# Attention with weighed outputs and turned tiles by VectorE and DMA, in an infini-attention plus mixer kernel on one core

## The chip, the core and the metric

The kernel runs on one core of a Trainium2 chip, as one launch. A core has TensorE (PE, matmuls and transposes into PSUM), VectorE (DVE), ScalarE (ACT), GpSimd (POOL), SyncE (SP), whose queue issues most of the DMAs here, and 16 DMA engines. Each engine runs its own instruction stream in order; semaphores tie the streams together. The metric is device time in microseconds for one run of the whole kernel, the median of the runs shown.

## The reference: what is computed

The input x has 2048 tokens of width 1024. First comes attention with a compressive memory, in four segments of 512 tokens and 32 heads of width 32, then a channel MLP. Cut to what matters:

```python
q, k, v = heads(layernorm(x) @ wq), ...          # 32 heads, 4 segments of L = 512
M, z = 0, 0
for s in range(4):
    p = softmax(qs @ ks.T * scale + mask)        # within the segment; mask adds -1e9 above the diagonal
    a_dot = p @ vs
    a_mem = (phi(qs) @ M) / (phi(qs) @ z + 1e-6) # phi(t) = t + 1 for t > 0, else exp(t)
    o_s = g * a_mem + (1 - g) * a_dot            # g = sigmoid(beta), one number a head
    M = M + phi(ks).T @ vs
    z = z + sum(phi(ks))
h = x + concat(o) @ wo
out = h + gelu(layernorm(layernorm(h)) @ w1 + b1) @ w2 + b2
```

A row of the softmax is divided by its sum. That division, and the factor (1 - g), can be applied to each probability or, later, to each output row p @ v: the result is the same.

## The kernel before, in words

The work goes through two halves of 1024 tokens; each half does attention (`attention`), the wo product (`wo_first`, `wo_second`) and the first product of the MLP (`Mixer`). The second product (`Second`) follows at the end. Everything is fp32, carried as a rounded upper part and a lower part (names ending in h and l), so that a product is three matmuls (`mm3`): high by high, high by low, low by high.

Attention of a half walks over 8 groups g of four heads and, inside, over 2 slices sl of 512 tokens. One (g, sl) is a unit: 16 units a half, 32 in all. A unit belongs to segment s = 2 * half + sl. Units with s > 0 read the memory, units with s < 3 update it, so 24 do each.

- `dense` is the projection part of a unit, as a generator of 24 steps: eight steps each for keys, queries and values (`project`), one `mm3` a step. It copies the results out of PSUM into halves (kh, kl, qh, ql), makes phi(keys) (pk) and phi(queries) (pq), and builds the operands of the logits with `stack`: for each of the four heads a 96-row tile of three 32-row blocks, each block copied from SBUF to SBUF by its own DMA, so 12 DMAs for keys and 12 for queries. `late`, which runs inside the next unit, turns the values on TensorE (vt to PSUM vn, then vs in halves), reads the memory (pm, then om), turns what it read on TensorE (om to pom, copied to omt), and updates the memory (pmm). phi(keys) is turned on TensorE too (pk to pkn).
- `heads` runs the softmax part of the unit before, one `slot` of six steps for each of its four heads. `PLAN` says which operations stand in which step: q0 to q3 the logits of the four row blocks (`qk`, with the exponential in `soft`), n the division of two row blocks (`norm`: a reciprocal on VectorE, then a product on GpSimd with the inverse sum and 1 - g), t the transposes of the probabilities on TensorE (`ptr`), s and S the lower halves (`sub`), a the product with the values (`av`), o the addition of its two parts into ot (`av_out`), and at the fourth head the memory's part omt and the store to o_dram. t works on the head one slot back, a on the one two slots back.
- `interleave` weaves the 24 steps of one unit's `dense` with the 24 steps of the previous unit's `heads`.
- `small` is a list of small matmuls (pm and pmm); `one_small` slips one of them in between others.
- `weights` loads wk, wq and wv of the next group (128 columns each) and splits them; `load_o` fetches the outputs of the other groups back from DRAM for the wo product. At the end of a half `last` runs the remaining `heads` beside `wo_first`.

The order of instructions on each engine in this stage isn't the order of the code. A planner goes through the code once, with costs of its own, and puts an instruction on its engine when its inputs and buffers are there by those costs; the place in the code is the priority. The resulting order is fixed before the run. Only some stages (`in_order`) and some single instructions (`behind`, `add_manual_dep`) are tied to the order of the code. Buffers matter to that order: stacks have 5 for each of keys and queries, rounded temporaries (tmpr) 6, plain ones (tmp) 5, PSUM tiles of tag d 3, qk 2, pt 2, av 1.

## Time and profile before

| | |
|---|---|
| Runs | 2302.54, 2303.82 and 2304.96 us; median 2303.82 |
| Profiled execution | span 2296.2 us from the first to the last instruction; its time from outside isn't given separately, the median lies 7.6 us above the span |
| TensorE | busy 2270.4 us, 99% of the span, granted clock 1.000 |
| DVE, ACT, POOL busy | 1540.3, 1225.0, 1092.4 us |
| DMA | 355.36 MB, mean 155 GB/s |
| Stages | attention about 30 to 530 us and 884 to 1400 us; first MLP product to 884 and 1736 us; second MLP product to the end |

How to read the lines that follow in the prediction: a group's row (line, engine, operation, output<-input, shape, count) gives busy microseconds, mean nanoseconds of one, then the idle time of that engine just ahead of these instructions and what ended it. A row of the timeline gives start and duration in microseconds. Matmuls are pipelined, so durations of neighbours on PE overlap, and the cost of one is the distance between starts. A row of a stretch gives its bounds and length, busy time and count of PE, PEld, DVE, ACT and POOL, the granted clock, the DMA share and GB/s. A DMA row gives the count, the size and the median time from issue to landing. SPq and ACTq are the queues of SP and ACT on which DMAs are issued.

### The profile page before, as it was taken

Reading aid. Unit: us, or ns where it says so; the run is one execution under the profiler, and the core shown is the slowest. Engines: PE = TensorE matmul, PEld = TensorE weight load, DVE = VectorE, ACT = ScalarE, POOL = GpSimd, SP = SyncE. Lnnn points to the kernel's source line nnn. Section 1 sums busy time; section 2 is a strip of 40 time slices with the busy share of each in tenths; the row PEclk is TensorE's granted clock in tenths of the full one; section 3 lists DMA queues with packets and bytes.
Section 4 is the critical chain, followed back from the end, with each engine's and each line's share of the span. In section 5 each row is a group of like instructions: output and inputs, shape, how many; then the busy total and the mean of one; then the engine's idle time right before and its main releaser. Section 6 shows DMA issues by size and latency. Waiting matters only on the chain.

```text
span 2296.2 us, 35279 instructions
## 1 busy us (share of the span) xinstructions
PE 2270.4 (99%) x11769; PEld 1890.8 (82%) x11769; DVE 1540.3 (67%) x3173; ACT 1225.0 (53%) x2549; POOL 1092.4 (48%) x1134
## 2 busy tenths in 40 slices
PE   8999999999999999999999999999999999999999
PEld 6888888878888888888888887888888888888887
DVE  6777777776655565777777777565566766577563
ACT  6777777775453445777777776363344223322221
POOL 5545555555244442555555556253445554155430
PEclk9999999999999999999999999999999999999999
DMA  6333333345465654433333344466667976476762
GB/s 190 92 85 91 93 89 85 87 120 182 139 204 172 188 165 142 113 91 86 85 87 88 87 111 140 156 211 175 176 188 263 345 243 216 159 253 221 249 234 90
DMA packets 322719, 355.36 MB, mean 155 GB/s; under 512 B 26190, under 2 KB 218730, under 8 KB 322538
## 3 DMA queue, kind: packets, MB, share of 16 engines
q1 hardware_dynamic: 259370, 316.40, 45.4%
q10 hardware_dynamic: 63168, 36.71, 5.3%
q8 instruction: 93, 1.52, 0.3%
q14 instruction: 88, 0.72, 0.1%
HBM read 226.59 MB, written 76.09 MB: 132 GB/s over the span
## 4 chain that ended last, share of the span: by engine, by line
PE 91%; ACT 3%; POOL 2%; DVE 2%; issue 1%; DMA 1%; ACTq 0%; SPq 0%; POOLq 0%; DVEq 0%
PE po L1278 22%; PE bps L882 9%; PE cps L882 7%; PE dps L882 6%; PE po L593 6%; PE ppt L573 6%; PE pqk L541 3%; PE vps L116 2%; PE vps L115 2%; PE kps L115 2%; PE kps L116 2%; PE vps L117 2%; PE kps L117 2%; PE pwo L117 2%; PE pwo L116 2%; PE pwo L115 2%
## 5 line engine op out<-in xcount | busy, mean ns | idle before, releaser
L557 POOL TENSOR_SCALAR pr<-pr,nm,gate 128x128 f32<-128x128 f32 (+3 forms) x512 | 322.6, 639 | 345.9 <-DVE nm L554 260.0
L550 ACT ACTIVATE pr<-pr,mx 128x256 f32<-128x256 f32 (+3 forms) x512 | 287.6, 562 | 161.9 <-DVE mx L542 158.2
L580 DVE TENSOR_TENSOR ptl<-ppt,pth 128x512 fp32r<-128x512 f32 (+1 forms) x384 | 227.2, 599 | 86.2 <-ACT pth L575 82.0
L542 DVE CUSTOM_DVE_ANT_0 pr<-pqk,mask 128x256 f32<-128x256 f32 (+3 forms) x512 | 243.3, 484 | 46.5 <-PE pqk L541 43.7
L573 PE MATMUL ppt<-ident,pr 128*128 128x128 f32 x1280 | 223.6, 277 | 2.1 <-POOL pr L557 1.4
L575 ACT CAST pth<-ppt 128x512 fp32r<-128x512 f32 (+1 forms) x384 | 194.2, 517 | 39.0 <-PE ppt L573 33.1
L1288 DVE TENSOR_TENSOR c<-c,po 128x512 f32<-128x512 f32 x160 | 105.4, 683 | 143.1 <-PE po L1278 135.5
L573 PEld LDWEIGHTS ppt<-ident,pr 128*128 128x128 f32 x1280 | 164.6, 140 | 32.5 <-POOL pr L557 2.6
L541 PE MATMUL pqk<-ks,qs 96*128 96x256 f32 (+3 forms) x512 | 161.3, 315 | 0.0
L92 POOL TENSOR_TENSOR wl<-wr,wh 128x1024 fp32r<-128x1024 f32 x52 | 124.5, 2393 | 70.8 <-PE pqk L541 27.6
L593 PE MATMUL po<-pth,vs 128*64 128x512 f32 (+3 forms) x512 | 155.4, 326 | 0.3 <-ACT pth L575 0.2
L593 PE MATMUL po<-ptl,vs 128*64 128x512 f32 (+3 forms) x512 | 153.9, 310 | 1.3 <-DVE ptl L580 1.2
L1278 PE MATMUL po<-w2h,zh 128*128 128x512 f32 x378 | 121.1, 390 | 0.8 <-DVE zh L1218 0.4
L1135 POOL TENSOR_TENSOR w2r<-w2r 128x512 f32<-128x512 f32 x54 | 85.4, 1593 | 72.0 <-DVE c L1288 36.9
L541 PEld LDWEIGHTS pqk<-ks,qs 96*128 96x128 f32 x512 | 96.2, 188 | 21.5
L994 POOL TENSOR_TENSOR s<-r 128x512 f32<-128x512 f32 x28 | 43.6, 1559 | 143.4 <-DVE sa L1010 87.1
L882 PE MATMUL bps<-zh,sb 128*128 128x512 f32 x336 | 111.0, 391 | 0.0
L882 PE MATMUL bps<-zh,sa 128*128 128x512 f32 x336 | 110.8, 390 | 0.0
L115 PE MATMUL vps<-yh,wh 128*128 128x512 f32 x256 | 109.4, 427 | 0.9 <-DVE MZ L497 0.9
L115 PE MATMUL kps<-yh,wh 128*128 128x512 f32 (+1 forms) x264 | 110.1, 417 | 0.0
L115 PE MATMUL qps<-yh,wh 128*128 128x512 f32 x256 | 106.8, 417 | 0.0
L1278 PE MATMUL po<-w2h,hl 128*128 128x512 f32 x322 | 103.2, 390 | 0.5 <-POOL hl L1218 0.3
(241 smaller groups left out, 6657.1 us busy)
## 6 DMA issues: line engine op xcount, KB each, us to landing
hr<-h_dram SPq DMA_DIRECT2D x112, 448.0 KB, 5.4
w2r<-in_B_w SPq DMA_DIRECT2D x122, 256.0 KB, 4.4
r<-in_B_w SPq DMA_DIRECT2D x56, 512.0 KB, 4.5
h_dram<-ht ACTq DMA_DIRECT2D x84, 256.0 KB, 3.7
ks<-kh SPq DMA_DIRECT2D x256, 64.0 KB, 2.0
qs<-qh SPq DMA_DIRECT2D x256, 64.0 KB, 2.0
wr<-in_A_wo SPq DMA_DIRECT2D x32, 512.0 KB, 4.0
wx<-in_B_w SPq DMA_DIRECT2D x56, 256.0 KB, 3.5
```

What stands on the lines that cost most here:

```text
L115: nc.tensor.matmul(ps, ah, bh, start=first, stop=False)
L116: nc.tensor.matmul(ps, ah, bl, start=False, stop=False)
L541: nc.tensor.matmul(pqk[:, :n], u["qs"][j][:, i * P:(i + 1) * P], u["ks"][j][:, 0:n], start=True, stop=True)
L542: nc.vector.tensor_tensor_reduce(out=st["pr"][:, offs[i]:offs[i] + n], in0=pqk[:, :n], in1=mask[:, 512 - n:512], op0=ALU.add, op1=ALU.min, ...
L550: nc.scalar.activation(pi, pi, AF.Exp, bias=mx[:, i:i + 1], scale=-1.0, accum_out=mx[:, 4 + i:5 + i])
L557: nc.gpsimd.tensor_scalar(pi, pi, nm[:, 4 + k:5 + k], gate[:, 1, 4 * g + j:4 * g + j + 1], op0=ALU.mult, op1=ALU.mult)
L573: nc.tensor.transpose(ppt[:, o:o + P], pr[:, offs[i] + jk * P:offs[i] + (jk + 1) * P], ident)
L575: acts["pth"] = n, nc.scalar.copy(pth[:, base:base + w], ppt[:, :w])
L580: nc.vector.tensor_tensor(o, x0, x1, op=ALU.subtract)
L593: nc.tensor.matmul(po[:, P * jk:], v, st[part][:, koff[jk]:koff[jk] + w], start=(jk, part) == (0, "pth"), stop=(jk, part) == (2, "ptl"))
L882: nc.tensor.matmul(ps, x_[:, c, :], y_[:, c, :], start=first and c == 0 and n == 0, stop=last and c == 3 and n == 2, skip_group_check=True)
L1278: nc.tensor.matmul(ps, x_[:, k], y_[k], start=opens and k == 0 and i == 0, stop=closes and k == self.KP - 1 and i == 2, skip_group_check=True)
```

## The change

Seven things are changed, all in attention.

1. The softmax isn't divided row by row any more. `norm` is gone; `inverse` (r) takes the reciprocals of a head's four row sums into rs and, at the fourth head, multiplies them by 1 - g on GpSimd. `weigh` (w) turns these 16 columns by one transpose on TensorE (pw), copies them out on ScalarE, stores them to DRAM and reads them back as a 128 x 512 tile in four broadcast loads. `av_out` multiplies the finished ot by it.
2. Values, phi(keys) and retrieved values aren't turned on TensorE any more. `turned` does a VectorE transpose of 32 x 32 blocks, one store to DRAM and four loads that put the blocks in place. The flags VT, KT and OT choose it, and all are on. The order of columns changes with it, so vs, pkh and pkl are indexed anew and omt is added through a rearranged view. The scratch for this lies in the two zt tiles that `wo_first` and `wo_second` use for weights.
3. `stack` stores the three blocks to one DRAM tile (three DMAs of 128 rows) and loads each head's 96 rows with one DMA: 7 DMAs in place of 12.
4. Lower halves of values and phi(keys) move from VectorE to GpSimd.
5. The output store stands at a step of its own (`out_store`, step 62), later than before.
6. Weights are loaded and split at steps (`load_weight`, `cast_weight`); the upper parts of wk and wv are cast on ScalarE, that of wq on VectorE.
7. `late` is gone. `TIMES` gives each operation of a unit a step, counted from the unit's first; 24 and above fall into the next units. `PLAN` is new.

The diff, cut to its core:

```diff
-PLAN = ('q1 S2', 'q0 n0 a0', 'q2 t0 a1', 'q3 n2 s0 o', 't1', 's1 t2')
+VT, KT, OT = True, True, True
+WLC = 8
+TIMES = dict(pk=10, kx=15, pkh=21, pkl=22, ks=16, qs=16, pq=16, pqh=20, pql=20, omt=20, vx=24, pm=25, vs=32, vl=33, pmm=40, om=35, omc=40, od=62, lk=13, lq=16, lv=20, ck=18, cq=22, cv=28)
+PLAN = ('r', 'q0', 'a0 S2 t0 q2 s0', 'a1 q1', 't1 w q3', 't2 o s1')
...
+    PKL, VSL, GTE, WHK, WHQ, WHV = nc.gpsimd, nc.gpsimd, nc.gpsimd, nc.scalar, nc.vector, nc.scalar
...
+        scr = [acts["zt"].tile([P, 4, 512], F32, tag=f"t{x_}3", name=f"sc{x_}") for x_ in "hl"]
+        def turned(src, to, mid):
+            nc.vector.transpose(mid.rearrange("p (c k d) -> p c k d", c=4, k=4), src.rearrange("p (k c d) -> p c k d", c=4, k=4))
+            d = turn_dram[acts.get("turned", 0) % len(turn_dram)]
+            acts["turned"] = acts.get("turned", 0) + 1
+            nc.sync.dma_start(d, mid)
+            for c in range(4):
+                nc.sync.dma_start(to[32 * c:32 * c + 32].rearrange("j (h x) -> j h x", h=4),
+                                  d[:, c * P:(c + 1) * P].rearrange("(h j) x -> j h x", h=4))
...
         def stack(a, b, name, order):
             out = []
+            n = acts[name] = acts.get(name, 0) + 1
+            d = s_dram[name][n % 2]
+            for blk, src in enumerate(order):
+                nc.sync.dma_start(d[:, blk], raw((a, b)[src]))
             for j in range(4):
                 st = ab.tile([96, 512], F32R, tag=name, name=name, bufs=5)
-                for blk, src in enumerate(order):
-                    nc.sync.dma_start(raw(st[32 * blk:32 * blk + 32, :]), raw((a, b)[src][32 * j:32 * j + 32, :]))
+                nc.sync.dma_start(raw(st), d[32 * j:32 * j + 32].rearrange("r b n -> (r b) n"))
                 out.append(st)
...
+            def key_turn():
+                v["kn"] = scr[1][:, 2 + sl]
+                turned(v["pk"], v["kn"], scr[1][:, 0])
+            def key_halves():
+                v["pkh"], v["pkl"] = tmpr("pkh"), tmpr("pkl")
+                v["pkn"] = v["kn"].rearrange("p (h k d) -> p k h d", h=4, k=4)
+                v["pk4"] = [x_.rearrange("p (k h d) -> p k h d", h=4, k=4) for x_ in (v["pkh"], v["pkl"])]
+                nc.scalar.copy(v["pk4"][0], v["pkn"])
+            def value_turn():
+                v["vn"] = scr[0][:, 2 + sl]
+                turned(ps["v"], v["vn"], scr[0][:, 0])
+            def memory_turn():
+                while v.get("read") != 1:
+                    one_small()
+                turned(v["om"], u["omt"], tmp("omx"))
...
-        def norm(st, i):
-            pr, mx, nm, j, g = st["pr"], st["mx"], st["nm"], st["j"], st["u"]["g"]
-            nc.vector.reciprocal(nm[:, 4 + i:6 + i], mx[:, 4 + i:6 + i])
-            for k in (i, i + 1):
-                pi = pr[:, offs[k]:offs[k] + P * (k + 1)]
-                nc.gpsimd.tensor_scalar(pi, pi, nm[:, 4 + k:5 + k], gate[:, 1, 4 * g + j:4 * g + j + 1],
-                                        op0=ALU.mult, op1=ALU.mult)
+        def inverse(st):
+            u, j = st["u"], st["j"]
+            if j == 0:
+                u["rs"] = ab.tile([P, P], F32, name="rs", bufs=1)
+            rs = u["rs"]
+            nc.vector.reciprocal(rs[:, 4 * j:4 * j + 4], st["mx"][:, 4:8])
+            if j == 3:
+                r4 = rs[:, 0:16].rearrange("p (h i) -> p h i", i=4)
+                GTE.tensor_tensor(r4, r4, gate[:, 1, 4 * u["g"]:4 * u["g"] + 4].unsqueeze(2).to_broadcast([P, 4, 4]),
+                                        op=ALU.mult)
+        def weigh(st):
+            u, j = st["u"], st["j"]
+            if j < 3:
+                return
+            n = acts["weighed"] = 1 - acts.get("weighed", 0)
+            w = u["w"] = tmp("w") if u["g"] == NG - 1 and u["s"] % 2 else scr[n][:, 1]
+            pw = ps_dense("pw")
+            nc.tensor.transpose(pw[0:16, 0:P], u["rs"][:, 0:16], ident)
+            nc.scalar.copy(w[0:16, 0:P], pw[0:16, 0:P])
+            d = r_dram[n]
+            nc.sync.dma_start(d, w[0:16, 0:P])
+            for k in range(4):
+                nc.sync.dma_start(w[32 * k:32 * k + 32, :],
+                                  bass.AP(tensor=d.tensor, offset=d.offset + 512 * k, ap=[[0, DH], [1, 512]]))
...
+                w = u["w"]
+                nc.gpsimd.tensor_tensor(w, ot, w, op=ALU.mult)
                 if u["omt"] is not None:
-                    nc.gpsimd.tensor_tensor(ot, ot, u["omt"], op=ALU.add)
-                if u["g"] < NG - 1:
-                    nc.sync.dma_start(o_dram[u["s"]][u["g"]], ot)
+                    if OT:
+                        w4 = w.rearrange("p (k c j) -> p k c j", k=4, c=4)
+                        nc.gpsimd.tensor_tensor(w4, w4, u["omt"].rearrange("p (c k j) -> p k c j", k=4, c=4), op=ALU.add)
...
+        def cast_weight(nxt, n):
+            wr = nxt[n]
+            wh, wl = nxt[n] = [wp.tile([P, DC, P], F32R, tag=f"w{x_}", name=f"w{x_}", bufs=3) for x_ in "hl"]
+            eng = {"k": WHK, "q": WHQ, "v": WHV}[n]
+            (nc.scalar.copy if eng is nc.scalar else eng.tensor_copy)(wh, wr)
+            for c in range(0, DC, WLC):
+                nc.gpsimd.tensor_tensor(wl[:, c:c + WLC], wr[:, c:c + WLC], raw(wh)[:, c:c + WLC], op=ALU.subtract)
...
         def last():
-            behind = acts.pop("late")
-            for _ in chain(heads(prev), tail()):
-                next(behind, None)
+            todo, base = acts.pop("todo"), acts.pop("unit") + 24
+            for t, _ in enumerate(chain(heads(prev), tail())):
+                for fn in todo.pop(base + t, ()):
+                    fn()
                 yield
```

310 lines of the change are left out of this document (185 added, 125 removed).

## The prediction

> **What bounds the kernel now.** I read the page's busy shares, then the chain that ended last, then busy time by stretches, because the change touches only attention (about 30 to 530 and 884 to 1400 us).
>
> ```profile
> PE 2270.4 (99%) x11769; PEld 1890.8 (82%) x11769; DVE 1540.3 (67%) x3173; ACT 1225.0 (53%) x2549; POOL 1092.4 (48%) x1134
> PE 91%; ACT 3%; POOL 2%; DVE 2%; issue 1%; DMA 1%; ACTq 0%; SPq 0%; POOLq 0%; DVEq 0%
> ...
> 30.00:493.00 463.00, 461.42 (x2797) 389.44 (x2796) 343.22 (x1007) 335.62 (x848) 238.49 (x336) 1.00 0.37 94
> 493.00:530.00 37.00, 33.22 (x194) 26.27 (x193) 28.62 (x78) 26.51 (x63) 20.90 (x25) 1.00 0.46 145
> 912.00:1363.00 451.00, 449.10 (x2741) 380.42 (x2741) 339.29 (x1016) 328.52 (x834) 252.72 (x337) 1.00 0.36 93
> 1363.00:1400.00 37.00, 34.07 (x193) 26.85 (x192) 28.97 (x79) 29.62 (x70) 22.74 (x24) 1.00 0.42 127
> ```
>
> The columns after the stretch are its length and the busy us of PE, PEld, DVE, ACT, POOL, then granted clock, DMA share and GB/s. In steady attention PE is idle 1.6 of 463 us and 1.9 of 451 us, at full clock; DVE is at 75%, ACT at 73%, POOL at 52 to 56%, DMA at 0.36. So attention costs what TensorE is given to do, and only instructions taken off TensorE pay. Where attention hands over to the wo blocks, PE is idle 3.8 and 2.9 us.
>
> The period, from two copies of a finished value projection, one pair of units (one group, both slices) apart:
>
> ```profile
> 251.53 0.59 ACT L461 COPY vt<-vps 128x512 f32<-128x512 f32 x1
> 313.43 0.59 ACT L461 COPY vt<-vps 128x512 f32<-128x512 f32 x1
> ```
>
> A pair takes 61.9 us, a unit 31, one of its 24 steps 1.29 us. There are 32 units.
>
> **What leaves TensorE.** The transposes of values (vn, all 32 units), phi(keys) (pkn, 24) and retrieved values (pom, 24), four to a unit:
>
> ```profile
> L516 PE MATMUL pom<-ident,om 128*128 128x128 f32 x96 | 19.3, 288 | 0.8 <-DVE om L484 0.8
> L469 PE MATMUL vn<-ident,vt 128*128 128x128 f32 x128 | 19.3, 273 | 0.6 <-ACT vt L461 0.6
> L453 PE MATMUL pkn<-ident,pk 128*128 128x128 f32 x96 | 14.4, 272 | 0.0
> ...
> 254.35 0.60 PE L469 MATMUL vn<-ident,vt 128*128 128x128 f32 x4
> 254.71 0.43 PE L541 MATMUL pqk<-ks,qs 96*128 96x384 f32 x1
> 254.97 0.60 PE L573 MATMUL ppt<-ident,pr 128*128 128x128 f32 x4
> ...
> 262.61 0.34 PE L541 MATMUL pqk<-ks,qs 96*128 96x384 f32 x1
> 262.79 0.23 PE L395 MATMUL pm<-mzl,pqh 128*128 128x132 f32 x1
> ...
> 266.21 0.27 PE L516 MATMUL pom<-ident,om 128*128 128x128 f32 x1
> 266.24 0.31 PE L395 MATMUL pmm<-vs,pkh 128*128 128x128 f32 x1
> 266.38 0.30 PE L516 MATMUL pom<-ident,om 128*128 128x128 f32 x1
> ```
>
> Durations overlap, so I count from start to start. Four transposes hold PE 0.36 us (254.35 to 254.71), and the pqk behind them takes 0.26 instead of the 0.18 it takes elsewhere (262.61 to 262.79): 0.44 us a group. A pom and the pmm beside it take 0.17; the pmm stays, so I give pom the same 0.11 each. 80 groups x 0.44 = 35.2 us. Added: one transpose pw a unit, bounded by 0 and a whole group; I take a quarter group and the penalty behind it, 0.11 + 0.09 = 0.2, x 32 = 6.4. **Net -28.8 us.** All of it lies on the path, since PE is never idle there.
>
> **What the other engines get.**
>
> ```profile
> L557 POOL TENSOR_SCALAR pr<-pr,nm,gate 128x128 f32<-128x128 f32 (+3 forms) x512 | 322.6, 639 | 345.9 <-DVE nm L554 260.0 <-PE qps L117 37.2 <-PE vps L117 13.2
> L607 POOL TENSOR_TENSOR ot<-ot,omt 128x512 f32<-128x512 f32 x24 | 30.9, 1287 | 27.4 <-DVE ot L604 27.4
> L472 DVE TENSOR_TENSOR vs<-vn,vs 128x512 fp32r<-128x512 f32 x32 | 22.0, 686 | 0.7 <-ACT vs L471 0.4 <-DMA qs<-qh 0.3
> L91 ACT CAST wh<-wr 128x1024 fp32r<-128x1024 f32 x18 | 18.9, 1049 | 13.6 <-DMA wr<-in_A_wo 6.7 <-PE pwo L117 2.3 <-PE kps L116 1.8
> ```
>
> POOL loses the 512 normalizations (322.6 us) and gets some 88 products and differences at 1.29 us (114 us: 32 output weights, 32 vs, 24 pkl) and 32 small gate products: about -195 us, and POOL leaves the softmax chain. ACT loses 56 copies at 0.59 us and gets 28 weight casts at 1.05 us and 32 small copies at perhaps 0.3: about +6 us. DVE loses 56 lower halves at 0.69 us, half its reciprocals and 28 casts, and gets 80 block transposes. No row shows one. I bound it by the tensor_scalar of POOL above, 0.64, and twice a DVE pass over 512 elements, 1.4, and take 0.69 as it is the same 512 elements on the same engine: 55 us in, 39 us and the casts and reciprocals out. At 1.4 it is at most +73 us over 960, DVE still under 85%. None of this sets the end; I cost it at nothing, covered by PE's 60 us a pair. If PE went, DVE would be next, at about 46 us a pair. The page Vector Engine (DVE) Microarchitecture Reference of the Trainium skill, section 3.8, has the transpose stream one element per cycle per lane, so no slower than an ordinary pass; the sum would be the same, and no row here shows it.
>
> **What the queues get.** This is where the change is paid.
>
> ```profile
> qs<-qh SPq DMA_DIRECT2D x256, 64.0 KB, 2.0
> o_dram<-ot SPq DMA_DIRECT2D x28, 256.0 KB, 2.3
> orr<-o_dram SPq DMA_DIRECT2D x28, 256.0 KB, 3.2
> ...
> 275.81 1.17 SPq L377 DMA_DIRECT2D qs<-qh  x2
> ...
> 282.94 0.59 SPq L377 DMA_DIRECT2D qs<-ql  x1
> ```
>
> Twelve stack copies hold SP from 275.81 to 283.53: 0.64 us each. Per unit SP issues 24 of them now. After: each stack is 3 stores and 4 loads (14 a unit), each turned tile a store and 4 loads (5; two or three tiles a unit), the weights of the outputs 5, store and weight loads 2.5: 31.5 or 36.5 issues, 20 to 23 us of a 30 us unit against 17 now. It fits, if SP does not stand idle between a store and the loads that read it. There are six such round trips in a busy unit (two stacks, three turned tiles, the weights).
>
> The tightest due time is that of the query stack, now first read one step later (q0 in step 1):
>
> ```profile
> 275.21 0.69 DVE L428 TENSOR_TENSOR ql<-qps,qh 128x512 fp32r<-128x512 f32 x1
> ...
> 284.77 0.22 PE L541 MATMUL pqk<-ks,qs 96*128 96x128 f32 x1
> ```
>
> From ql done (275.9) to step 1 of the next unit (284.8) are 8.9 us. The new path is three issues (the last 1.3 us in), 2.3 us to land, a load, 3.2 us to land: 6.8 us. On a free queue it is 2.1 us early. Behind everything that stands ahead of it in program order (the four loads of the turned key, a weight load, seven of the key stack: 12 x 0.64 = 7.7 us) it is 5.6 us late. Which end applies is the planner's order, and the trace shows what it does:
>
> ```profile
> 251.43 0.53 SPq L326 DMA_DIRECT2D wr<-in_A_wk  x1
> ...
> 266.82 0.59 SPq L377 DMA_DIRECT2D ks<-kh  x1
> 267.51 0.53 SPq L609 DMA_DIRECT2D o_dram<-ot  x1
> ...
> 273.94 0.51 SPq L377 DMA_DIRECT2D ks<-kh  x1
> ```
>
> The load of wk stands behind both units of the pair in the code and is issued 62 us ahead of that place; an output store goes between the third and fourth key stack, which waits for a buffer. So instructions go when their inputs and buffers are there, not where they are written, and kh, kl and pk are there 6 to 9 us before ql. I take the free-queue end for most units and charge +4 us in all for the units whose stacks stand behind a weight load (14 x 0.3).
>
> The handover: the split wo weights of k = 3 live in zt, which attention now uses as scratch until the output of (7, 0) is done, step 11 of the tail.
>
> ```profile
> 500.99 0.48 PE L115 MATMUL pwo<-wh,oh 128*128 128x512 f32 x1
> ...
> 512.67 0.45 PE L115 MATMUL pwo<-zh,oh 128*128 128x512 f32 x1
> ```
>
> Now they are used 11.7 us after the first wo matmul. Twelve tail steps at 1.4 us, then product, sum and split put them at about 24 us; other wo blocks and the tail's heads cover part of the 12 us. Bounds 0 and 8 us a half; I take 3, as PE is idle there about 3 us already: +6 us.
>
> **Sum.** -28.8 + 4 + 6 = **-18.8 us**. The profiled span is 2296.2; the runs' median 2303.82 lies 7.6 above it, which I leave as it is. 2303.8 - 18.8 = **2285**.
>
> **Rivals.**
> *SP's round trips arrive late (slower).* Loads wait on SP for the store to land:
>
> ```profile
> SPq L1171 <- DMA s_dram<-hr: 71.5, 12, 7.7
> ```
>
> In the last stage 12 such waits held SP 6.0 us each, with nothing issued behind them. If the six trips of a busy unit each hold it for 1.7 us (2.3 less its issue), SP needs 23.4 + 10.2 = 33.6 us of a 30 us unit; then pqk waits in step 1 on TensorE and the projections stand behind it. 3.6 us in each of the 16 units with three turned tiles is 58 us: +58 - 28.8 + 6 gives 2339. It decides above 0.6 us a unit. For it: the DMA share rises from 0.36 to perhaps 0.65, so landings lengthen; against: the free order above. The Trainium skill, page DMA: Bandwidth & Descriptors, section "Two DMAs through the same engine are not ordered", says one queue does not order a load behind a store, so the issuer must wait for the store's completion; the trace agrees with its 6.0 us waits. By that rule none of these waits can go away, and if all stand idle the time is this rival's 2339.
>
> *ScalarE waits for a turned tile (slower).* kx stands at 15, its halves at 21: 7.7 us for a chain of 0.7 + 2.3 + 4 x 0.64 + 3.2 = 8.8, and the exps queue behind the cast. 24 units x 1.8 us = +43 on my sum: 2328. Against: pk is ready at step 11, and the planner may turn it then.
>
> *It saves nothing.* Lateness of 0.6 us a unit gives back the gain: 2304.
>
> **Chances.** Mine 0.52, with its own range 2264 to 2300 (no lateness and a free handover: 2275, and up to 10 us less if the idle 1.6, 1.9, 3.8 and 2.9 us close too). SP late 0.25, ScalarE late 0.15, nothing saved 0.08, of which 0.06 fall within 0.2% (4.6 us, what a measurement of this kernel can tell) and 0.02 above. So faster 0.52, same 0.06, slower 0.42. The ends above reach 5.6 us x 32 late, some 2450, but half of SP's rival lies under 2350; the range is 2264 to 2350.
>
> **What would show it.** Right: no vn, pkn, pom; PE idle under 1% in attention; a pair at 60 us; POOL near 900 us. Wrong: pqk waiting for a DMA into qs or ks, pkh or vs idle on a DMA on ScalarE, PE under 97% of the steady stretch, or more than 8 us idle at a handover.

## The result, and the profile after

The changed kernel takes 2331.99 us (median, 2326.8 to 2334.28) against 2304.39 of the kernel before beside it: a ratio of 1.0125 (95% interval 1.0107 to 1.0143), slower where 2285 was forecast. The profiled execution took 2326.8 us, the shortest of the four; its span is 2324.9. From the page of the changed kernel, the busy shares and the chain that ended last:

```profile
PE 2257.8 (97%) x11481; PEld 1863.1 (80%) x11481; DVE 1516.8 (65%) x3041; ACT 1232.6 (53%) x2553; POOL 887.5 (38%) x742
...
PE 73%; DMA 11%; DVE 4%; ACT 4%; POOL 3%; issue 2%; SPq 2%; ACTq 0%; POOLq 0%; DVEq 0%
```

TensorE is 12.6 us less busy than before (2270.4), and idle for 67.1 us of the span instead of 25.8: 41.3 more. The difference is the 28.7 us by which the span grew. DMA, which held 1% of the chain, holds 11%. The same stretches of attention as were shown of before (length, busy us of PE, PEld, DVE, ACT, POOL, granted clock, DMA share, GB/s):

```profile
30.00:493.00 463.00, 444.12 (x2604) 365.95 (x2603) 329.44 (x920) 333.48 (x835) 146.92 (x154) 0.99 0.62 190
493.00:530.00 37.00, 32.00 (x185) 26.46 (x184) 27.07 (x75) 26.63 (x65) 14.65 (x15) 0.95 0.72 217
912.00:1363.00 451.00, 440.04 (x2584) 365.24 (x2582) 325.06 (x931) 330.82 (x819) 156.25 (x161) 1.00 0.64 196
1363.00:1400.00 37.00, 34.75 (x214) 29.08 (x215) 29.54 (x84) 28.22 (x68) 13.67 (x13) 1.00 0.74 238
```

Steady attention, which had 1.6 and 1.9 us of idle TensorE, has 18.9 and 11.0. The waits of TensorE (engine, line, who ended them: us in all, times, longest):

```profile
PE pqk L651 <- DMA qs<-qs_dram: 25.3, 18, 3.3
...
PE pqk L651 <- DVE ptl L708: 7.2, 7, 1.6
PE pwo L123 <- POOL zl L99: 4.9, 3, 2.5
PE pwo L122 <- ACT zh L98: 3.4, 2, 2.1
```

The first row is what the prediction named as the sign that it is wrong: the pairs (pqk) wait for the load of the query stack. One of the 18, from the timeline of the changed kernel (start, us, instruction; in brackets how long the engine was idle before it, and who ended that):

```profile
1104.63 0.69 DVE L484 TENSOR_TENSOR ql<-qps,qh 128x512 fp32r<-128x512 f32 x1
...
1104.99 0.38 SPq L366 DMA_DIRECT2D turn_dram<-scl  x1
1105.46 2.72 SPq L399 DMA_DIRECT2D ks<-ks_dram  x3
...
1108.71 1.74 SPq L368 DMA_DIRECT2D scl<-turn_dram  x4
...
1110.50 0.43 SPq L399 DMA_DIRECT2D ks<-ks_dram  x1
1111.04 1.04 SPq L396 DMA_DIRECT2D qs_dram<-qh  x2
...
1112.19 0.39 SPq L396 DMA_DIRECT2D qs_dram<-ql  x1
1115.74 1.74 SPq L399 DMA_DIRECT2D qs<-qs_dram  x4
...
1118.51 0.30 PE L651 MATMUL pqk<-ks,qs 96*128 96x128 f32 x1 [2.37 <-DMA qs<-qs_dram]
```

The halves of the queries are ready at 1105.3, but their stores go out from 1111.04 on. Ahead of them on SP stand loads of the key stack and the four loads of the turned key tile, which wait until that tile's store (1104.99) has landed. So the stores lie 5.7 us behind their data, the load follows 3.5 us later, and TensorE stands 2.37 us. Of the 5.7 us, SP's listed waits are 1.3 (0.5 for the landing of the turned tile, 0.8 for buffers of the key stack); most of the rest is the issue of the eight loads themselves. Between the query stores and their load, 3.0 us are the wait for the landing.

A long gap costs more than its length. Stretches of 2 us of the changed kernel around a wait of 3.0 us:

```profile
162.00:164.00 2.00, 0.48 (x3) 0.04 (x1) 1.56 (x4) 1.07 (x3) 0.21 (x1) 1.00 0.08 15
164.00:166.00 2.00, 0.55 (x2) 0.58 (x3) 0.07 (x1) 0.00 (x0) 0.00 (x0) 0.63 0.95 247
166.00:168.00 2.00, 2.00 (x6) 1.20 (x6) 0.23 (x2) 0.49 (x2) 0.00 (x0) 0.50 0.72 253
168.00:170.00 2.00, 2.00 (x9) 1.81 (x8) 0.02 (x1) 0.34 (x1) 0.00 (x0) 0.50 0.09 28
170.00:172.00 2.00, 2.00 (x10) 1.55 (x10) 1.30 (x4) 1.22 (x4) 0.00 (x0) 0.66 0.42 117
```

The granted clock falls to 0.50 during the gap and is back at 172. Over stretches of 4 us, one minus the clock adds up to 12.0 us in the changed kernel, at six places (two in attention, four at the handovers), and to nothing in the kernel before; the first 20 us and the last stretch of each program are left out. The Trainium skill, page TensorE: Matmul & The Clock Gate, part 1, has the clock at half rate after an idle window of about 3.4 us until a busy window of as much; the trace agrees in kind but not in size: a gap of 3.0 us was enough, and the clock was low for some 6 us behind it.

By stage, every kernel of this study. A half of attention ends with the first wo matmul (pwo), the handover with the first matmul of the MLP (cps); the second half begins with its first kps. MLP and rest hardly move (274 and 809 to 813 us). A ratio is against the runs of the kernel before beside that kernel, whose medians lie from 2299.4 to 2304.4; "over before" is the difference of the two medians, and kernels are compared by it below, because a difference of medians from different groups of runs would carry up to 5 us of that spread. Times of stages are from the profiled execution alone, which can lie beside the median: 5.2 us under it in the changed kernel and 3.4 in 14, 5.0 over it in 1, 5.8 in 13 and 6.4 in 17, so a few us between stages of two kernels can be the execution's:

| kernel | median us | over before | ratio (95%) | att. 1 | handover 1 | att. 2 | handover 2 |
|---|---|---|---|---|---|---|---|
| before | 2304.4 | 0 | 1 | 501.0 | 114.1 | 484.6 | 111.8 |
| after | 2332.0 | 27.6 | 1.0107–1.0143 | 510.4 | 124.0 | 483.5 | 120.8 |
| 1 turns on TensorE | 2333.6 | 31.8 | 1.0120–1.0154 | 502.5 | 126.3 | 497.5 | 124.4 |
| 2 SBUF stacks | 2458.2 | 156.5 | 1.0659–1.0696 | 595.5 | 112.3 | 551.1 | 107.7 |
| 3 last group free of scratch | 2326.3 | 24.6 | 1.0083–1.0118 | 514.3 | 121.0 | 487.9 | 117.8 |
| 4 turns on GpSimd's queue | 2435.3 | 133.5 | 1.0548–1.0601 | 554.9 | 132.5 | 535.3 | 124.4 |
| 5 old order | 2342.9 | 43.3 | 1.0167–1.0214 | 523.2 | 116.4 | 495.5 | 122.5 |
| 6 query stack first | 2347.3 | 47.7 | 1.0185–1.0219 | 522.3 | 126.9 | 484.3 | 125.5 |
| 7 = 1 + old order | 2324.9 | 25.3 | 1.0090–1.0122 | 508.0 | 119.0 | 492.1 | 119.0 |
| 8 = 7 + old weighing | 2316.1 | 16.6 | 1.0047–1.0092 | 500.1 | 118.6 | 491.5 | 118.8 |
| 8b old order, old weighing | 2356.2 | 56.8 | 1.0221–1.0260 | 530.1 | 120.5 | 493.9 | 121.0 |
| 9 stores by ScalarE | 2332.1 | 32.7 | 1.0116–1.0162 | 516.3 | 124.7 | 484.4 | 118.5 |
| 10 = 8 + stores at once | 2313.3 | 12.1 | 1.0036–1.0070 | 500.4 | 120.6 | 489.1 | 116.8 |
| 11 = 8 + loads as before | 2327.1 | 25.9 | 1.0093–1.0124 | 507.6 | 119.1 | 494.0 | 119.2 |
| 12 = 8 + SBUF stacks | 2305.2 | 4.0 | 0.9998–1.0019 | 496.6 | 117.0 | 488.4 | 116.7 |
| 13 = 8 + read values turned | 2303.6 | 2.4 | 0.9995–1.0018 | 500.5 | 118.3 | 486.2 | 116.4 |
| 14 = 12 + free scratch | 2298.4 | -3.1 | 0.9976–0.9994 | 495.7 | 116.2 | 486.9 | 111.1 |
| 15 = 14 + read values turned, stores at once | 2297.9 | -3.6 | 0.9972–0.9989 | 493.6 | 114.5 | 487.7 | 114.1 |
| 17 = 9 + later halves | 2332.4 | 29.8 | 1.0107–1.0141 | 517.7 | 123.0 | 488.7 | 121.1 |

### The profile page after: what moved, and what is told of

Read it like the earlier page. It is cut to its first block, busy times and chain, and to the rows that moved or that the text cites. A ratio compares the mean times of both kernels' runs of the same rounds, so it can differ in the third digit from the quotient of the medians.

```text
span 2324.9 us, 34571 instructions
## 1 busy us (share of the span) xinstructions
PE 2257.8 (97%) x11481; PEld 1863.1 (80%) x11481; DVE 1516.8 (65%) x3041; ACT 1232.6 (53%) x2553; POOL 887.5 (38%) x742
## 4 chain that ended last, share of the span: by engine, by line
PE 73%; DMA 11%; DVE 4%; ACT 4%; POOL 3%; issue 2%; SPq 2%; ACTq 0%; POOLq 0%; DVEq 0%
PE po L1431 19%; PE bps L1035 9%; PE cps L1035 7%; PE dps L1035 6%; PE po L721 4%; PE ppt L701 4%; DMA qs_dram<-ql 3%; PE pqk L651 3%; PE qps L122 2%; PE qps L123 2%; PE qps L124 2%; DMA qs<-qs_dram 2%; PE kps L122 2%; PE kps L123 2%; PE pwo L123 2%
## 5 line engine op out<-in xcount | busy, mean ns | idle before, releaser
L660 ACT ACTIVATE pr<-pr,mx 128x128 f32<-128x128 f32 (+3 forms) x512 | 289.0, 564 | 147.5 <-DVE mx L652 143.2
L652 DVE CUSTOM_DVE_ANT_0 pr<-pqk,mask 128x128 f32<-128x128 f32 (+3 forms) x512 | 246.4, 482 | 107.0 <-PE pqk L651 102.6
L651 PE MATMUL pqk<-ks,qs 96*128 96x128 f32 (+3 forms) x512 | 183.5, 360 | 34.5 <-DMA qs<-qs_dram 25.3
L794 POOL TENSOR_TENSOR wl<-wr,wh 128x1024 fp32r<-128x1024 f32 x42 | 100.3, 2388 | 189.9 <-ACT wh L792 156.4
L721 PE MATMUL po<-pth,vs 128*64 128x512 f32 (+3 forms) x512 | 148.1, 310 | 0.7 <-POOL vs L531 0.7
L123 PE MATMUL kps<-yl,wh 128*128 128x512 f32 (+1 forms) x264 | 102.9, 390 | 0.1
L124 PE MATMUL kps<-yh,wl 128*128 128x512 f32 (+1 forms) x264 | 102.8, 389 | 0.0
```

Of the source, the lines that this page charges most:

```text
L123: nc.tensor.matmul(ps, ah, bl, start=False, stop=False)
L124: acts["mm"] = nc.tensor.matmul(ps, al, bh, start=False, stop=last)
L651: nc.tensor.matmul(pqk[:, :n], u["qs"][j][:, i * P:(i + 1) * P], u["ks"][j][:, 0:n], start=True, stop=True)
L652: nc.vector.tensor_tensor_reduce(out=st["pr"][:, offs[i]:offs[i] + n], in0=pqk[:, :n], in1=mask[:, 512 - n:512], op0=ALU.add, op1=ALU.min, ...
L660: nc.scalar.activation(pi, pi, AF.Exp, bias=mx[:, i:i + 1], scale=-1.0, accum_out=mx[:, 4 + i:5 + i])
L721: nc.tensor.matmul(po[:, P * jk:], v, st[part][:, koff[jk]:koff[jk] + w], start=(jk, part) == (0, "pth"), stop=(jk, part) == (2, "ptl"))
```

## The experiments

Theory A: SP takes its DMAs strictly in order, so a round trip that waits for its landing holds what stands behind it, and the query stack is the first to be late.

**1. The three turns on TensorE again.**

```diff
-VT, KT, OT = True, True, True
+VT, KT, OT = False, False, False
-    ... VSL ... = nc.gpsimd
+    ... VSL ... = nc.vector
```

> The changed kernel with the three turned tiles back on TensorE (VT, KT and OT off, so vn, pkn and pom return, and the lower half of the values goes back to VectorE because it is read from PSUM); the weighing of the outputs, the stacks by DRAM rows, the late stores and the new steps stay. Theory A (SP stands between a store and its loads, so the query stack lands late): SP loses 12.5 issues and two or three round trips a unit, pqk's waits for qs fall from 25 us to under 8, the two attention parts keep TensorE idle under 1%, but TensorE gets 35 us of transposes back; attention about 1000 us, as long as or a little shorter than in the changed kernel (994), total 2315 to 2335. Theory B (the sheer DMA traffic lengthens landings): traffic falls by a quarter, waits halve only. Rival C (the new order of steps itself is slow): TensorE's idle time stays as it is and the total rises by the 35 us, to about 2365.

The waits on the query stack fell from 25.3 to 4.1 us, as theory A had it, and the time stayed: 2333.6, 31.8 us over before against 27.6, with intervals that overlap. So the turned tiles cost nearly as much as they save. The two halves of attention, first here, then in the changed kernel, then in the kernel before:

```profile
30.00:502.50 472.50, 471.10 (x2857) 396.22 (x2856) 335.89 (x946) 358.65 (x888) 120.26 (x135) 1.00 0.50 155
903.10:1400.60 497.50, 488.39 (x2920) 408.14 (x2919) 345.25 (x985) 371.94 (x906) 143.30 (x152) 1.00 0.50 154
```

```profile
30.00:510.40 480.40, 461.12 (x2705) 380.06 (x2703) 342.86 (x956) 346.65 (x867) 158.03 (x164) 0.99 0.63 192
908.60:1392.10 483.50, 471.17 (x2768) 391.05 (x2768) 349.68 (x998) 354.95 (x875) 171.63 (x174) 1.00 0.65 198
```

```profile
30.00:501.00 471.00, 468.52 (x2835) 394.73 (x2833) 349.63 (x1024) 342.14 (x864) 244.53 (x342) 1.00 0.37 95
889.40:1374.00 484.60, 480.99 (x2907) 405.69 (x2906) 359.94 (x1060) 353.61 (x880) 267.40 (x360) 1.00 0.37 97
```

With the turned tiles TensorE's work in the second half is 17.2 us less, as the 40 groups x 0.44 us of the prediction have it (17.6), and its idle time 3.2 more. In the first half the same two figures are -10.0 and +17.9; without the 2.95 us that half clock adds to the work there (busy time of half-us stretches times one minus their clock) the fall is 12.9. But the kernel before has only 468.5 and 481.0 us of TensorE work in the two halves: the rest of the change adds 2.6 and 7.4, with 1.7 us of half clock in the latter.

**2. Both stacks by SBUF to SBUF copies**, twelve each as in the kernel before.

```diff
-            for blk, src in enumerate(order):
-                nc.sync.dma_start(d[:, blk], raw((a, b)[src]))
...
-                nc.sync.dma_start(raw(st), d[32 * j:32 * j + 32].rearrange("r b n -> (r b) n"))
+                for blk, src in enumerate(order):
+                    nc.sync.dma_start(raw(st[32 * blk:32 * blk + 32, :]), raw((a, b)[src][32 * j:32 * j + 32, :]))
```

> The changed kernel with stacks as before: twelve copies from SBUF to SBUF, with no store and no wait in between; all else changed. Theory A: two of the round trips of every unit go, the query stack waits only for its own issues; pqk's waits for qs under 8 us, attention 10 to 20 us shorter, total 2305 to 2320. Rival (SP is short of issue time, not stuck in waits): ten more issues a unit make it worse, total over 2335.

2458.2 us, the side of the rival. SP has 24 issues of 0.59 us for 14 of about 0.4, and from 1000 to 1300 us its waits add up to 83 us where they were 147. That it is short of issue time is still only argued: 39 of the 83 us it stands in front of GpSimd's outputs. TensorE's waits, mostly on GpSimd's lower halves of the values and on the outputs' sum:

```profile
PE po L718 <- POOL vs L528: 20.9, 20, 2.4
PE po L718 <- DVE ot L729: 18.7, 23, 2.3
```

The handovers are short (112.3 and 107.7) although the scratch lies in zt here too, so the scratch by itself need not make a handover late.

**3. The last group free of the scratch**: its values and phi(keys) turned on TensorE, its outputs in tmp tiles.

```diff
-                VSL.tensor_tensor(...)
+                (VSL if g < NG - 1 else nc.vector).tensor_tensor(...)
...
-                if KT:
+                if KT and g < NG - 1:
...
-            if VT:
+            if VT and g < NG - 1:
...
-            w = u["w"] = tmp("w") if u["g"] == NG - 1 and u["s"] % 2 else scr[n][:, 1]
+            w = u["w"] = tmp("w") if u["g"] == NG - 1 else scr[n][:, 1]
```

> The changed kernel, but in the last group of each half values and phi(keys) are turned on TensorE and both output weights lie in ordinary temporaries, so that the zt tiles are free for the wo weights before the handover. Theory (the handover's extra 9.9 and 9.0 us come from wo weights that wait for the scratch): first wo matmul to first cps matmul falls from 124 and 121 us back to 112 to 116, total 2312 to 2320. Rival (the handover is late because of the longer DMA landings and the output weights' round trip): it stays at 120 or more, total 2330.

Handovers 121.0 and 117.8: in these executions 3 us each of the 10 and 9 are the scratch, between the theory and its rival.

**4. The turned tiles' DMAs issued by GpSimd** (the store and four loads in `turned` by `nc.gpsimd` for `nc.sync`).

> The changed kernel with the stores and loads of the turned tiles issued by GpSimd in place of SP; same bytes, same destinations. Theory A: SP no longer stands in those waits, so the query stack goes out when it is ready; pqk's waits for qs fall from 25 us to under 5, attention is 15 to 25 us shorter, total 2305 to 2320. Theory B (traffic): same bytes, so landings and waits stay; total within 5 us of the changed kernel. Rival (GpSimd itself becomes late, because it stands in the waits): its lower halves and weight halves come late and the total rises above 2340.

```profile
PE ppt L701 <- ACT pr L660: 37.6, 15, 4.0
...
PE pqk L651 <- DMA qs<-qs_dram: 8.8, 6, 4.4
```

The rival came true (2435.3 us). The query stack is nearly in time (8.8 us), but the turned tiles come later still: GpSimd, from 30 to 550 us, stands 77 us in front of landings, and ScalarE 85 us in front of the tiles:

```profile
POOL sch L368 <- DMA turn_dram<-sch: 41.1, 15, 4.5
...
POOL scl L368 <- DMA turn_dram<-scl: 36.0, 9, 6.5
```

```profile
ACT pkh L464 <- DMA scl<-turn_dram: 46.2, 9, 9.0
ACT vs L527 <- DMA sch<-turn_dram: 38.5, 7, 6.1
```

**5. and 7. The old order of the steps in a slot**, in the changed kernel (5) and with the turns on TensorE (7).

```diff
-PLAN = ('r', 'q0', 'a0 S2 t0 q2 s0', 'a1 q1', 't1 w q3', 't2 o s1')
+PLAN = ('q1 r S2', 'q0 a0', 'q2 t0 a1', 'q3 w s0 o', 't1', 's1 t2')
```

> One part of the change is undone: the steps of a head slot stand as in the kernel before (second pair first, transposes in steps 3, 5 and 6), with the weighing's two new steps put where the old norms stood. In the changed kernel's second attention half the account reads: before 484.6 us, TensorE busy 481.0 of it; with all turns on TensorE again 488.4 busy, 7.4 more than before, where the weighing was priced at 3.2 a half; with the turned tiles 471.2 busy and 12.3 idle. Theory (the new order of the steps costs TensorE some 4 us a half, because a pair that follows transposes takes 0.48 us for 0.39): busy time of the second half falls from 471.2 to about 467, and the first pairs, asked for one step earlier, wait longer for the query stack, so the waits of the pairs on its landing rise from 25 us to 30 to 40; the sum comes out within 8 us of 2332. Rival (the order only moves which matmul pays after a transpose, there being three groups a slot either way): busy stays at 470 to 472, and only the waits change.

> All three turns are on TensorE again (as in the first experiment), and the steps of a slot stand in the old order too: what is left of the change is the weighing, the stacks by DRAM rows, the late stores and the placing of the loads. Theory (order costs TensorE some 4 us a half): second attention half 497.5 falls to about 492, TensorE busy in it from 488.4 to about 484, time 2322 to 2328. Rival (order costs nothing; the 7.4 us of TensorE time beyond the kernel before are the weighing itself and the matmuls behind it): half 2 stays at 496 to 499 and the time at 2331 to 2336.

With the turns on TensorE the old order is better by 6.5 us (25.3 over before against 31.8): TensorE's work falls from 488.4 to 485.0 us in the second half and from 471.1 to 469.2 in the first, and the handovers by 7.3 and 5.4. With the turned tiles by DMA it is worse by 15.7 (43.3 against 27.6). The waits on the query stack are more often but not longer in sum (24 waits, 25.2 us, against 18 and 25.3); what is new are waits of the second products on ScalarE's pth (11.2 us) and VectorE's ptl (6.6) and of the transposes on ptl (8.3). TensorE's work in the second half is 472.4, where the theory had 467. So the theory of the order held for 7 and missed for 5, and why the feeding engines are later in 5 is not shown.

**6. The query stack ahead of the turned key tile.**

```diff
-... kx=15, pkh=21, pkl=22, ks=16, ...
+... kx=17, pkh=23, pkl=24, ks=9, ...
```

> The steps that issue DMAs are placed anew: the key stack at 9 instead of 16, the turn of phi(key) at 17 instead of 15 and its halves two later, so that on the SP queue the query stack's three stores no longer stand behind the landing of the turned key tile. Nothing else is changed. Theory A (head of line on SP: the stores of the query stack are late because SP stands in a wait for another tile's landing): waits of the pairs on the query stack fall from 25 us to under 8, the clock of the attention goes to 1.00, attention halves fall by some 6 us each, and the time to 2310 to 2320. Rival B (the DMA engines are crowded, 0.62 of their time, and a store and a load of the stack take 3.6 and 4.1 us wherever they stand): the waits stay at 20 us or more and the time at 2328 to 2334. Rival C (the key tile is now the late one): the waits move to the halves of phi(key) or to the memory update, and the time stays above 2325.

Rival C, and more of it than expected: 2347.3. TensorE's waits, then those of ScalarE from 30 to 520 us:

```profile
PE ppt L701 <- ACT pr L660: 20.5, 9, 3.9
PE pqk L651 <- DMA qs<-qs_dram: 10.1, 5, 4.6
```

```profile
ACT vs L527 <- DMA sch<-turn_dram: 27.9, 7, 5.3
ACT pkh L464 <- DMA scl<-turn_dram: 18.9, 8, 3.4
```

The waits on the query stack fall from 25.3 to 10.1, but ScalarE stands 46.8 us in front of turned values and keys (18.6 from 30 to 500 us in the changed kernel), the exponentials behind those casts are late, and TensorE waits for them. The gaps are long: one minus the clock adds up to 25.6 us. That the late exponentials come from the casts in front of them is read from these two lists, not tried.

**8. and 8b. The old weighing** (GpSimd scales the probabilities, old order), with the turns on TensorE (8) and with the turned tiles by DMA (8b).

```diff
-            ops = {..., "r": (p1, inverse), "w": (p1, weigh), ...
+            ops = {..., "n": (cur, norm), ...
...
-                nc.gpsimd.tensor_tensor(w, ot, w, op=ALU.mult)
...
-                    nc.gpsimd.tensor_tensor(w, w, u["omt"], op=ALU.add)
+                    nc.gpsimd.tensor_tensor(w, ot, u["omt"], op=ALU.add)
```

> From the kernel of the seventh experiment (turns on TensorE, old order of the steps: 2324.9 us, handovers 119.0 and 119.0 us, second half of attention 492.1) the weighing of the outputs is taken out as well: GpSimd weighs the probabilities as in the kernel before. Left of the change are the stacks by DRAM rows, the late stores of the outputs, the scratch and the placing of the loads. Theory (the weighing, through its round trip for the last units and its transposes, makes the handover late and adds TensorE work): handovers back to 112 to 115 us, the second half of attention to about 486, time 2304 to 2312. Rival (the handover is late because of the late stores, the scratch or the loads' placing): handovers stay at 117 to 120, time 2318 to 2325. Rival (the stacks by DRAM rows alone cost the attention): handover back, attention halves stay at 492 and more than 505, time about 2315.

> The changed kernel with one part undone: the probabilities are weighed by GpSimd before the transposes, in the old order of the steps; the turned tiles by DMA stay, and so do the stacks. The SP queue loses one of its six round trips a unit: five issues and, by the waits of SP in 300 us of the second half, 21.8 us before the weights' store, 14.3 us for its landing. Theory A (SP's order makes the query stack late): the pairs' waits on the query stack fall from 25 us to 10 to 15, handovers to 114 to 118, time 2310 to 2325. Rival (GpSimd, now with some 200 us more of work, makes the lower halves of the turned tiles late): waits of the second products on vs and of the probabilities' transposes on GpSimd appear, time above 2335.

8 gains 9 us (2316.1), nearly all in the first half of attention; the handovers stay at 118.6 and 118.8, so their lateness is not the weighing's. TensorE's work falls by 2.2 and 2.0 us, but 1.9 and 1.7 us of that are half clock, which 7 has in its attention and 8 has not: for the transposes of the weights, priced at 3.2 a half, 0.3 a half is left. 8b is 40 us slower than 8. There the query stack is not the main wait (6.8 us), and neither is GpSimd (4.8 us of waits on the probabilities, 1.6 on vs). By the waits it looks like the rival that the prediction had as ScalarE waiting for a turned tile. Its waits from 30 to 500 us, and then TensorE's:

```profile
ACT vs L527 <- DMA sch<-turn_dram: 27.0, 8, 4.8
```

```profile
PE po L704 <- ACT pth L686: 21.4, 14, 2.8
PE ppt L684 <- DVE ptl L691: 16.7, 11, 2.1
```

**9. The stacks' stores by ScalarE**, behind its own casts (`nc.scalar.dma_start(d[:, blk], ...)` in `stack`).

> The changed kernel with the six stores of the two stacks issued by ScalarE behind its own casts, in place of SP; the loads of the stacks and all other DMAs stay on SP. Theory A (the stores stand on SP behind other tiles' waits): query stores go out right behind the cast and the subtraction, some 3 to 5 us sooner; the pairs' waits on the query stack fall from 25 us to under 10 and the attention halves by 5 to 8 us each; ScalarE pays 6 x 0.37 us a unit (the duration of its DMA issues elsewhere in the kernel), 2.2 us of some 8 it has idle a unit: time 2312 to 2325. Rival B (the loads, still on SP behind other waits, or the crowded DMA engines set the landing): waits stay at 18 us or more, time 2328 to 2340. Rival C (ScalarE becomes late by the issues): waits of the transposes on the softmax tile (pr) grow, time above 2335.

The stack is in time (3.7 us of waits left), and the time is 2332.1, no shorter (32.7 us over before against 27.6, with intervals that overlap). TensorE's waits, then ScalarE's from 30 to 516 us:

```profile
PE pqk L651 <- DVE mx L652: 10.3, 4, 4.2
...
PE ppt L701 <- DVE ptl L708: 8.8, 9, 1.9
...
PE pqk L651 <- DMA qs<-qs_dram: 3.7, 7, 1.2
```

```profile
ACT pkh L464 <- DMA scl<-turn_dram: 24.1, 7, 4.8
ACT vs L527 <- DMA sch<-turn_dram: 18.3, 10, 2.8
```

ScalarE, which now issues the stores, stands 13.2 us more in front of transfers of the stacks in this window. So the query stack's lateness is shown to be SP's order, and shown not to be the whole cost: put right, it leaves ScalarE standing. Whether ScalarE was the next in line or is late by what it was given here, the experiment does not separate.

**17. The halves of the turned tiles later** than in 9.

```diff
-... pkh=21, pkl=22, ... vs=32, vl=33, ...
+... pkh=30, pkl=31, ... vs=35, vl=36, ...
```

> From the kernel of the ninth experiment (the changed kernel with the stacks' stores issued by ScalarE: 2332.1 us; the query stack is in time there, 3.7 us of waits, but ScalarE stands 38 us of the second half and 50 of the first in front of turned key and value tiles): the halves of the turned tiles are taken later, phi(key) at steps 30 and 31 instead of 21 and 22, values at 35 and 36 instead of 32 and 33. The memory update at 40 and the first second product at about 38 are their users. Theory A (what is left is ScalarE standing in program order in front of tiles on their way): ScalarE's waits on scratch tiles fall under 12 us a half, TensorE's waits on DVE and ScalarE fall by 8 to 10 us in all, attention 500 to 506 and 474 to 478 us, time 2305 to 2318. Rival (the tiles are late in themselves, SP being full: later halves only hand the wait to the second products): waits of the second products on vs appear, time 2328 to 2340.

Inconclusive, because the edit did not do what it meant. One cast of phi(key), in 9 and here:

```profile
1116.06 0.62 ACT L464 CAST pkh<-scl 128x512 fp32r<-128x512 f32 x1 [0.56 <-DMA scl<-turn_dram]
```

```profile
1118.96 0.62 ACT L464 CAST pkh<-scl 128x512 fp32r<-128x512 f32 x1 [0.37 <-DMA scl<-turn_dram]
```

Nine steps are some 12 us, but the cast stands 2.9 us later, and still in front of its tile. Most of the 2.9 is ScalarE as a whole, which is 2.5 us later at this place; in the order of the instructions the cast moved by one, behind the next copy of ot. So the step did not set the order here; the planner, which places an instruction by when it takes its inputs to be there, is the likely reason. ScalarE's waits on the two tiles are 43.3 us in the first half (42.4 in 9).

**10, 11, 12 and 13: one part each, from kernel 8.** 10 stores the outputs at once; 11 issues the weights' loads and casts as before (`ws = weights(g + 1)` at the end of a pair); 12 has the SBUF stacks of experiment 2; 13 turns the read values alone by VectorE and DMA (`VT, KT, OT = False, False, True`).

> From the kernel of the eighth experiment (turns on TensorE, GpSimd weighs the probabilities, old order; 2316.1 us, handovers 118.6 and 118.8 us against 114.1 and 111.8 before): the stores of the outputs are issued at once when a unit ends, as in the kernel before, in place of 62 steps later. Theory (late stores cost the handover, because the reloads of the outputs stand behind them on SP): handovers back to 112 to 115 us, time 2305 to 2310. Rival (they cost nothing): handovers stay at 117 to 120, time 2312 to 2319.

> From the eighth experiment's kernel: the weights' loads and casts of the next group are issued as in the kernel before (all three at the end of a pair of units), in place of at steps 13 to 28 of the second unit. Theory (the new placing of the weights' loads, casts and lower halves makes the wo chain at the handover start late): handovers back to 112 to 115, time 2305 to 2310. Rival: handovers stay at 117 to 120 and the time at 2312 to 2319, or the attention gets slower where the casts run in a bunch.

> From the eighth experiment's kernel: both stacks are built by twelve SBUF to SBUF copies a stack as in the kernel before, so SP has 24 issues of 0.59 us a unit for 14 of 0.38 to 0.43, and 302 KB a stack less go through DRAM. What is left of the change is the late stores, the scratch and the placing of the loads. Theory (the DRAM rows, by the traffic of 101 MB more or by their landings on SP, make the other loads late at the handover): handovers back to 112 to 115 us, time 2303 to 2309. Rival (the stacks are not the cause): handovers 117 to 120, time 2312 to 2320.

> From the eighth experiment's kernel: only the values read from the memory are turned by VectorE and DMA, the other two turns stay on TensorE. Nothing on ScalarE or TensorE waits for this tile: GpSimd adds it to the outputs at the end of the unit. TensorE loses 15 groups of four transposes a half, 9.2 us of busy time by the names' rows in the second half, some 4.5 us by their pitch. Theory A (a turned tile costs by whom it makes wait in program order; this one makes nobody wait but SP): attention 3 to 5 us shorter a half, time 2306 to 2312. Rival (any further round trip on SP makes the query stack late): waits of the pairs on the stack grow from 2.6 us to over 10, time 2316 to 2330.

By how far each lies over before, against the 16.6 us of 8: the late stores cost 4.5 us, with intervals that overlap, and do not make the handover. The new placing of the weights' loads is a gain: without it 9.3 us more. The stacks by DRAM rows cost 12.6 us (12 lies 4.0 over), in the profiled executions 3.5 and 3.1 in the halves and 1.6 and 2.1 in the handovers; 12 moves 50 MB less than 8, not the 101 of the expectation, which are those of the whole change. The read values turned by DMA gain 14.2 us (13 lies 2.4 over), more than the 4 to 10 expected. The profiled execution of 13 is the longest of its ten, 5.8 us over their median, and gains only 6.7 us of span (2314.3 to 2307.6). In it TensorE's work falls by 2.1 and 6.1 us, with 6.3 us at half clock in its attention where 8 has none, and the waits on the query stack grow from 2.6 to 10.0 us, the sign that the rival named, though the rival's time did not come. What the shorter executions gain is in no profile.

**14 and 15: put together.** 14 is 12 with the outputs of the last group in tmp tiles; 15 turns the read values by DMA as well and stores the outputs at once.

> From the kernel with turns on TensorE, the old weighing, the old order and SBUF to SBUF stacks (2305.2 us, handovers 117.0 and 116.7 against 114.1 and 111.8 before): the outputs of both units of the last group lie in the tmp tiles, so the zt tiles that take the last quarter of wo are free from the seventh group's stores on. Theory (what is left at the handover is that scratch): handovers 113 to 115 us, time 2298 to 2302. Rival (the placing of the loads and casts, or the stores, are what is left): handovers 116 to 118, time 2303 to 2307.

> The last kernel with the read values alone turned by VectorE and DMA and with the outputs stored at once. Theory A (a turned tile pays where nobody on the path stands in front of it, and the stacks by SBUF copies have no landing between store and load): TensorE loses 9 us of busy time a half by the rows, some 4 to 5 us of pitch; attention halves 492 to 495 and 481 to 484, time 2290 to 2298, under the kernel before by 0.1 to 0.5%. Rival (SP, with 24 issues of 0.59 us for the stacks and five more for the turn, becomes late): waits of the pairs on the stacks return, time 2303 to 2320.

Both are faster than the kernel before, by 0.15 and 0.19% (intervals 0.06 to 0.24 and 0.11 to 0.28). The scratch is 7.1 us (4.0 over before to 3.1 under), and the second handover is back at 111.1. The turned tile, with the stores at once, gains nothing clear of noise here, against the theory. The second half of attention, 14 and then 15:

```profile
886.20:1373.10 486.90, 482.49 (x2908) 407.69 (x2906) 353.91 (x1047) 361.16 (x895) 266.12 (x361) 1.00 0.37 97
```

```profile
882.40:1370.10 487.70, 477.53 (x2846) 398.99 (x2845) 358.26 (x1062) 356.78 (x880) 265.62 (x360) 1.00 0.42 111
```

TensorE works 5.0 us less in it and is idle 5.8 us more. In the first half it works 2.1 us less, and the half is 2.1 shorter. From 930 to 1370 us of 15 it waits for the engines that feed it:

```profile
PE po L700 <- DVE ptl L687: 3.3, 8, 1.0
PE po L700 <- ACT pth L682: 2.5, 6, 0.4
PE ppt L680 <- DVE ptl L687: 2.4, 3, 1.0
```

A further variant, with only the key stack by DRAM rows and else as 15, gives results other than the reference's, for a reason not found; its time is not used.

## Why the prediction was wrong

**What leaves TensorE: right in the main.** 0.44 us a group held in the second half, 17.2 us against 17.6; in the first it was 12.9 without half clock. The turn on VectorE took 0.70 us against 0.69 taken, GpSimd is at 887.5 us against 900, and VectorE, ScalarE and GpSimd did not run out of time in sum.

**What is added to TensorE: too small.** pw was priced at 6.4 us, the new order of the steps and the clock at nothing. From 8 to 1, weighing and new order together add 9.5 us of TensorE work in attention, 7.8 without half clock (4.2 and 5.3, or 0.7 and 7.1 without); how they share it is uncertain. Attention of the changed kernel has 4.7 us more of busy time by half clock, and outside attention TensorE is busy 4.6 us longer, where the other four places of low clock lie. The sum of the busy time: the turned tiles -30.2 without half clock (1 to the changed kernel; -35.2 forecast), the rest of the change in attention +8.3 (before to 1; +6.4 forecast), +4.7 and +4.6, make -12.6, which is the page's.

**The query stack: the step that failed.** It was charged at +4 us in all, 14 units at 0.3 us, and no row stands behind the 0.3; TensorE waited 25.3 us for it, 18 times. The prediction took the end of a free queue, 2.1 us early, because a weight load was issued 62 us ahead of its place in the code. That row shows how the planner writes the stream of SP, not that SP passes over what must wait: at run time SP takes its stream in order. The other end, 5.6 us late, was nearer: in the place shown the stores lie 5.7 us behind their data, and TensorE waits 2.37. The landings were mis-sized too: 2.3 us for the store and 3.2 for the load were taken, 3.6 (qs_dram<-ql) and 4.1 are the medians in the changed kernel, 2.2 more and so the whole margin of the free queue.

**The rival that came true, by another reason.** Its 2339 is near the measured 2332, but it was priced as SP running out of time (33.6 us in a unit of 30), so that the nearness is luck. Its 23.4 us of issues took 0.64 us for each; the issues between SBUF and DRAM measured 0.31 to 0.43. From 1000 to 1300 us the waits of SP add up to 147 us in the changed kernel and to 150 in the kernel before: SP has as much time to spare as ever. What counts is which tile stands behind which wait and behind which loads. Each cure moved the cost on: with SP's order changed (6) or the stores on ScalarE (9) the stack waits less (10.1 and 3.7 us) and ScalarE stands; on GpSimd's queue (4), GpSimd and ScalarE stand. That the rival of ScalarE was not another case but the next in line is argued from this, not shown by itself. It was priced at 1.8 us a unit, where its own chain, 8.8 against 7.7, gives 1.1.

**The handover: +18.9 instead of +6.** The scratch was sized rightly: 3 us a half in experiment 3, 6.4 in the two handovers of 14 against 12. The rest was missing. Along 12, 8, 7, 1 and the changed kernel the two handovers together go by +7.8 against before (late stores, placing, scratch), +3.7 (DRAM rows), +0.6 (weighing), +12.7 (new order) and -5.9 (turned tiles): 18.9. Some of the 12.7 can be the execution's, as 1 is shown in its longest of four. Why the new order costs time there was not tried; that it ends the last output two steps of the tail later is only argued.

**By parts, over before:** 12 lies 4.0 us over, the DRAM rows add 12.6, the weighing 8.7, the new order 6.5, and the turned tiles take off 4.2: 27.6 (the intervals are some 4 us wide to each side, so the last is not clear of noise). What the turned tiles do depends on what they meet: -4.2 in the new order, +18.0 in the old one (5 against 7), +40.2 with the old weighing (8b against 8). What stays open is what 13 gains beside its TensorE work, and whether ScalarE's standing can be removed, as 17 did not reach it.

## What to carry to other kernels

A tile that is turned through DRAM costs nothing on the engine that it leaves, but a store and a load that waits for it stand in an in-order queue: write down what is queued behind that wait, and behind the wait of the engine that reads the tile, before counting the gain. Spare time of SP said nothing on this here (147 us and 150); the position of its issues and waits did. And work taken off TensorE, the bound, can turn into waits on the engines that feed it: in the second half of experiment 15, 5.0 us less work went with 5.8 us more of idle time.

## What was not expected of the hardware

A wait of TensorE of 3.0 us was followed by some 6 us at a granted clock of 0.50 to 0.66, so that this gap cost about twice its length (one minus the clock adds up to 12.0 us in the whole changed kernel and to 25.6 in experiment 6). A DMA issue between SBUF and DRAM held SP for 0.31 to 0.43 us (medians by tile in the changed kernel's attention), an SBUF to SBUF copy for 0.59. With the DMA share at 0.62 instead of 0.37, loads of 512 KB landed later: wk in 6.5 us instead of 4.4, wv in 5.2 instead of 4.4, wq in 4.7 instead of 4.2.
